# Square roots of ten chunks in pairs, four widths for the tail units, and a pair unit at the end

## The chip, the core and the metric

The kernel runs on one core of one Trainium2 chip. The metric is the device time of one execution in microseconds (us). TensorE (PE) multiplies into PSUM, ScalarE (ACT) applies functions and copies, VectorE (DVE) does element-wise work and scans, GpSimd (POOL) issues the scattered writes, SyncE (SP) issues the other transfers. Every engine has a queue of its own and takes its instructions in the order in which they stand there.

## What is computed

```python
a_base = sigmoid(a_param)
a_t = exp(8 * sigmoid(r_gate) * log(clip(a_base)))
x_gated = sqrt(max(1 - a_t * a_t, 1e-6)) * sigmoid(i_gate) * x
h_t = a_t * h_(t-1) + x_gated          # along 3648 steps, 4 sequences, 256 channels: y
group  = argmax(y @ w_group)           # 4 groups
expert = argmax(y @ w_expert[group])   # 4 experts in each: 16
out = weight_of_both_softmaxes * (relu(y @ w1[group, expert]) @ w2[group, expert])
```

There are 14592 tokens of 256 channels; w1 is 256 x 1024 and w2 1024 x 256 for each of the 16 experts. A gated recurrence is scanned along time, and every token of its result goes through the one expert that a two-level router picks. Which expert that is stands in the data, so units of work take their expert and their rows from tables that the kernel makes as it runs.

## The kernel before

The program is not written in the order in which it runs. Functions such as `add_chunk` (the recurrence and the router of one chunk) and `add_unit` (an expert's two products for a group of rows) hand operations to a planner, each with its engine, a cost, a due time and the operations that it comes after. `plan.run` then emits the operations one by one: per engine, of those that can start about first, the one with the earliest due time. So a due time moves an operation against all others of its engine.

**Chunks.** The tokens pass in 16 chunks (sizes 4, 13 times 8, 4 and 2 blocks of 128 tokens), planned 16.5 us apart. With channels on partitions, there are two halves `h` of 128 channels. On ACT a chunk goes through tanh (`tanh_r`, L352), the exponential (`decay`, L357), the square (`square`, L365), the square root (`norm`, L371, both halves at once) and the input gate's tanh (`gate_i`, L375). tanh, exp and square are in one function table of ACT, the square root in another, so that the planner's order has a table load ahead of a root and one behind it, on the next tanh or exp. DVE then scales (`scale_s`, L383) and scans (`scan`, L394). PE turns the result into rows with the router's logits beside them (`rows1`), which ACT copies out of PSUM (`rows2`, L419) and POOL scatters to DRAM (L520), sorted by expert. The buffers `v` that hold squares and roots are four, two for a chunk.

**Units.** The rows of an expert are served in units. Eight resident blocks (L1154, L1170) and 12 "native" units run while chunks still pass. After these come 14 units of two blocks (256 rows) from tables made early, then 11 pair units from the table `tP` (two blocks each) and last 16 tails from the table `tT`, one for each expert, with two or three blocks that end at the expert's last row. A unit's four steps `j` have 12 products with W1 into PSUM (`mm1`, for a tail `mm1_tail`; three products for each of two halves of the channels, with high and low parts of the operands), the ReLU on ACT (L942) and its low part on DVE (L945), and then products with W2 into `q_o` (`mm2`). PE takes mm1 of step j ahead of mm2 of step j - 1. In a tail each of these is made for three blocks and for two, and the value `has3` picks one on each engine (`tail_if`, L965, behind one register load per engine and tail, L964). At the end of a unit `finish` scales each block out of `q_o`, on ACT and DVE, and `give` scatters it to the output (L1036, POOL). The tail of expert 15 is the last unit; its last step goes block by block, and its three results are planned as block 2, 0, 1.

Of the kernel before, what the change touches and what calls it, by code (L numbers as in the profile page):

```python
# [158 lines left out]
def rglru_moe_kernel(ctx: ExitStack, tc: tile.TileContext, x, r_gate, i_gate, a_param,  # L159
# [48 lines left out]
    ORES = 60  # L208
    HALVED = (2, 3, 4)
# [3 lines left out]
    IF = 0.3  # L213

# [354 lines left out]
    def add_chunk(ck, before):  # L569
# [11 lines left out]
        sq = {}  # L581
        for h in range(2):
# [5 lines left out]
        n2 = op("ACT", 2 * act(W), lambda: norm(ck), due + ONORM, [sq[0], sq[1]], use=[b["v", 0], b["v", 1]], table="sqrt",  # L588
# [15 lines left out]

        urgent = SOON if ck.c in URGENT else 0.0
# [203 lines left out]
    def tails():  # L809
# [34 lines left out]
    class Unit:  # L844
        def __init__(self, u, tb, t, due):
# [5 lines left out]
            self.final = tb is tT and t == NE - 1  # L851
            self.always = tb is tT or t < 2 or u < NATIVE + 2
# [8 lines left out]
    def load_weights(m, k):  # L861
# [11 lines left out]
        pool = "wf" if m.tb is tT else "x"  # L873
# [26 lines left out]
    def gather(m):  # L900
# [4 lines left out]
        if m.nb == 3:  # L905
            m.g = m.g[:, ::-1]

# [3 lines left out]
    def prep1(m, c):  # L911
        m.qx = pools["q_r"].tile([P, 512], F32, name="q_r")
        for h in range(m.nb):
            T.transpose(m.qx[:, h * P:(h + 1) * P], m.g[:, h, c * X1:c * X1 + P], ident)  # L914
# [32 lines left out]
    def mm1(m, j):  # L947
        m.qh = pools["q_h"].tile([P, 512], F32, name="q_h")
        for f in range(2):
            w1_products(m, j, f, m.qh[:, f * TS:(f + 1) * TS], TS)  # L950
# [20 lines left out]
    def mm1_tail(m, j):  # L971
# [6 lines left out]
        def body(N):  # L978
            for f in range(2):
                w1_products(m, j, f, q[f][:, :N], N)  # L980
        tail_if(m, ENG.PE, lambda: body(3 * P), lambda: body(2 * P))
        return q

    def relu_hi_tail(m, j, q):
        m.hh[j] = [pools["a"].tile([P, CH * P], F32, name="a").bitcast(F32R) for f in range(2)]

        def body(N):
            for f in range(2):
                relu1(m.hh[j][f][:, :N], q[f][:, :N])
        tail_if(m, ENG.Activation, lambda: body(3 * P), lambda: body(2 * P))  # L990

    def relu_lo_tail(m, j, q):
        m.hl[j] = [pools["i"].tile([P, CH * P], F32, name="i").bitcast(F32R) for f in range(2)]

        def body(N):
            for f in range(2):
                relu2(m.hl[j][f][:, :N], m.hh[j][f][:, :N], q[f][:, :N])
# [3 lines left out]
    def w2_products(m, j, hs):  # L1001
        tail = m.nb == 3
        steps = [(n, h) for n in range(3) for h in hs]
        if m.final and j == J - 1:
            steps = [(n, h) for h in sorted(hs, key=lambda h: (h + 1) % 3) for n in range(3)]
        for n, h in steps:
            for f in range(2):
                hx, w = (m.hl if n == 2 else m.hh)[j], (w2h, w2l, w2h)[n]
                mv = hx[f][:, h * P:(h + 1) * P] if tail else hx[:, f * TS + h * P:f * TS + (h + 1) * P]
# [218 lines left out]

    def add_results(m, bqs, due):
        for h in (2, 0, 1) if m.final else range(m.nb):  # L1230
            b = buf("o")
            bq = bqs[0]
            if h == 2:
                f_ = op("DVE", 0.5, lambda: finish(m, 2), due - HASTE, m.p2[-1:] + [m.oc], [b], [bq, m.bc])
            else:
# [270 lines left out]
```

## Time and profile before

| | |
|---|---|
| time, median of 3 runs | 898.94 us (898.26 to 898.94) |
| the profiled execution | 905.73 us, span 903.9 us |
| PE busy | 835.9 us (92%), 6288 matmuls |
| DVE busy | 661.9 us (73%) |
| ACT busy | 606.7 us (67%) |
| POOL busy | 288.3 us (32%) |

Busy times are unions of spans. Matmuls are pipelined: they start about 0.117 us (256 columns) apart and each is shown with a span of 0.28 us, so PE counts as busy over a gap of up to some 0.16 us, and a group is best timed from the start of its first matmul to the start of the next group. A wait is shown with the instruction that ended it. The last copy of a chunk's rows on ACT starts at 336.7 us, and the first tail's matmuls at 646 us.

### The profile page before, as it was taken

How to read it: one execution, taken by the hardware profiler on the slowest of the kernel's cores; microseconds unless marked ns; L12 is line 12 of the kernel's file. 1: busy time of each engine (PE TensorE's matmuls, PEld its weight loads, DVE VectorE, ACT ScalarE, POOL GpSimd, SP SyncE). 2: the span in 40 equal slices, each digit the busy share in tenths (PEclk: the TensorE clock that was granted, in tenths of full speed). 3: DMA queues.
4: the chain of work that ended last, by engine and by line, in shares of the span. 5: the costliest groups of instructions: out<-in, count | busy, mean ns of one | idle time of the engine just before them, and what ended most of it. 6: DMA issues, size and time to landing. Idle time of an engine off the chain costs nothing.

```text
span 903.9 us, 18963 instructions
## 1 busy us (share of the span) xinstructions
PE 835.9 (92%) x6288; PEld 809.3 (90%) x6288; DVE 661.9 (73%) x1351; ACT 606.7 (67%) x903; POOL 288.3 (32%) x290
## 2 busy tenths in 40 slices
PE   1459889999989989999999999999999999999994
PEld 1358779999879979999999999999999999999994
DVE  5897889888878846787777777778766666666671
ACT  9997989999879735655665555566555555555551
POOL 2326443663772557311111111111212212121132
PEclk9758999999999999999999999999999999999998
DMA  9998868999885677867777767788655656555420
GB/s 306 409 414 314 309 197 283 394 389 353 282 298 173 227 250 239 262 199 249 233 235 234 236 219 232 228 281 270 212 178 166 187 182 198 155 172 177 135 72 23
DMA packets 74462, 216.28 MB, mean 239 GB/s; under 512 B 10709, under 2 KB 28895, under 8 KB 71776
## 3 DMA queue, kind: packets, MB, share of 16 engines
q1 hardware_dynamic: 62464, 183.61, 61.6%
q0 software_dynamic: 11872, 31.10, 9.0%
q8 instruction: 66, 1.08, 0.5%
q14 instruction: 60, 0.49, 0.2%
HBM read 182.76 MB, written 34.00 MB: 240 GB/s over the span
## 4 chain that ended last, share of the span: by engine, by line
PE 77%; issue 5%; POOL 2%; ACT 1%; DVE 1%; DMA 0%; POOLq 0%; DVEq 0%; ACTq 0%
PE q_o L253 36%; PE q_h L253 29%; PE q_y L253 9%; PE q_r L914 2%; POOL out_dram L1036 1%; PE q_r L1108 0%; POOL y_s L520 0%; DMA y_s<-wf,pi 0%; ACT a L352 0%; ACT hh L1124 0%; ACT o L1028 0%; DVE o L1032 0%; ACT wf L419 0%; DVE v L383 0%; ACT a L357 0%
## 5 line engine op out<-in xcount | busy, mean ns | idle before, releaser
L1036 POOL DMA_INDIRECT out_dram<-o,cl x122 | 134.6, 1103 | 442.8 <-ACT o L1028 242.7
L253 PE MATMUL q_h<-xh,w1h 128*128 128x256 f32 (+1 forms) x720 | 186.6, 287 | 0.2 <-issue 0.2
L253 PE MATMUL q_h<-xh,w1l 128*128 128x256 f32 x592 | 164.7, 278 | 0.5 <-issue 0.5
L253 PE MATMUL q_h<-xl,w1h 128*128 128x256 f32 x592 | 164.5, 278 | 0.3 <-issue 0.3
L520 POOL DMA_INDIRECT y_s<-wf,pi x114 | 133.6, 1172 | 82.5 <-issue 35.0
L253 PE MATMUL q_o<-w2h,hh 128*128 128x256 f32 x784 | 156.5, 332 | 1.9 <-ACT hh L1124 1.3
L253 PEld LDWEIGHTS q_o<-w2h,hh 128*128 128x128 f32 x784 | 123.5, 189 | 10.1 <-ACT hh L1124 1.5
L253 PEld LDWEIGHTS q_h<-xh,w1h 128*128 128x128 f32 x720 | 126.8, 189 | 1.9 <-PE q_o L253 1.3
L942 ACT ACTIVATE hh<-q_h 128x512 fp32r<-128x512 f32 x100 | 60.1, 601 | 88.7 <-PE q_h L253 77.2
L253 PEld LDWEIGHTS q_h<-xh,w1l 128*128 128x128 f32 x592 | 111.1, 188 | 1.1 <-issue 1.1
L253 PEld LDWEIGHTS q_h<-xl,w1h 128*128 128x128 f32 x592 | 111.4, 188 | 0.7 <-issue 0.3
L945 DVE SCALAR_TENSOR_TENSOR hl<-q_h,hh 128x512 fp32r<-128x512 f32 x100 | 68.7, 688 | 46.6 <-ACT hh L942 44.9
L253 PE MATMUL q_y<-yw,a 128*128 128x148 f32 x360 | 60.8, 315 | 33.6 <-DVE a L394 25.1
L253 PEld LDWEIGHTS q_y<-yw,a 128*128 128x128 f32 x360 | 54.5, 208 | 38.7 <-issue 20.7
L253 PE MATMUL q_o<-w2l,hh 128*128 128x256 f32 x464 | 77.7, 293 | 1.1 <-ACT wf L419 1.0
L394 DVE TENSOR_TENSOR_SCAN a<-a,v 128x1024 f32<-128x1024 f32 (+8 forms) x44 | 68.9, 1581 | 0.4
L253 PEld LDWEIGHTS q_o<-w2l,hh 128*128 128x128 f32 x464 | 65.2, 189 | 2.8 <-ACT wf L419 1.2
L893 DVE TENSOR_TENSOR w1l<-x,w1h 128x1024 fp32r<-128x1024 f32 x50 | 61.0, 1221 | 6.3 <-ACT w1h L891 3.8
L942 ACT ACTIVATE a<-q_y 128x384 fp32r<-128x384 f32 (+1 forms) x64 | 25.0, 442 | 58.3 <-issue 32.8
L253 PE MATMUL q_o<-w2h,hl 128*128 128x256 f32 x400 | 62.9, 279 | 0.6 <-DVE hl L945 0.6
L893 DVE TENSOR_TENSOR w2l<-x,w2h 128x1024 fp32r<-128x1024 f32 x50 | 60.6, 1218 | 2.2 <-ACT w2h L891 2.2
L253 PE MATMUL q_h<-x,w1h 128*128 128x384 f32 (+1 forms) x256 | 58.7, 318 | 0.0
(300 smaller groups left out, 1846.5 us busy)
## 6 DMA issues: line engine op xcount, KB each, us to landing
x<-in_moe_w_dram SPq DMA_DIRECT2D x100, 512.0 KB
wf<-in_moe_w_dram SPq DMA_DIRECT2D x64, 512.0 KB
w2h<-in_moe_w_dram SPq DMA_DIRECT2D x14, 1024.0 KB
a<-in_r_gate_dram SPq DMA_DIRECT2D x26, 512.0 KB
i<-in_i_gate_dram SPq DMA_DIRECT2D x26, 512.0 KB
x<-in_x_dram SPq DMA_DIRECT2D x26, 512.0 KB
w2l<-in_moe_w_dram SPq DMA_DIRECT2D x24, 512.0 KB
g<-y_s SPq DMA_DIRECT2D x37, 276.0 KB
```

The lines of the kernel that those rows point to most:

```text
L253: last[0] = T.matmul(*a, **k).ins.name
L394: V.tensor_tensor_scan(a[:, sl], a[:, sl], v[:, sl], init, ALU.mult, ALU.add)
L520: ins = G.indirect_dma_start(out=y_s, out_offset=bass.IndirectOffsetOnAxis(ap=ck.pi[:, k:k + 1], axis=0), in_=ck.t["yo", k // 4][:, k % 4, ...
L893: V.tensor_tensor(lo[m.b][:, sl], src, hi[m.b][:, sl].bitcast(F32), op=ALU.subtract)
L914: T.transpose(m.qx[:, h * P:(h + 1) * P], m.g[:, h, c * X1:c * X1 + P], ident)
L942: S.activation(hh, q, AF.Relu)
L945: V.scalar_tensor_tensor(hl, q, 0.0, hh.bitcast(F32), op0=ALU.max, op1=ALU.subtract)
L1036: ins = G.indirect_dma_start(out=out, out_offset=bass.IndirectOffsetOnAxis(ap=m.col("idx", h), axis=0), in_=m.o[h], in_offset=None, bounds ...
```

## The change

Three things are changed. First, chunks 5, 7, 9, 11 and 13 get the due times of their recurrence 8 us later, and the chunk behind each of them gets its own 8 us sooner; besides, the square root of the first chunk of a pair may only be placed once both squares of the second are placed. Rows and routing of the first chunk are due 8 us later too, those of the second as before; loads keep their due times.

Second, a tail holds its rows at the end of its 384 columns, the empty ones ahead of them (`m.at`), and how many are empty is kept in a table `room`. PE loads that number at a tail's first step and picks the columns of the W1 products by it: with 128 or more empty rows the last 256 columns; else the first product over all 384, and the other five from column 0, 32, 64 or 96 on. ACT and DVE still choose between two and three blocks. The chain of DVE that makes the tails' tables is due 150 us later.

Third, the last pair unit comes behind the tails. It always loads its weights, into the tails' buffers `wf`, and its last step is two operations of PE, one for each block, with the block's result and scatter placed right after each.

```diff
+    PAIRS, SOONER, LATER = (5, 7, 9, 11, 13), 8, 8
+    TRIM = 32
+    LATE = 150
...
         sq = {}
+        mid = due
+        due += (ck.c in PAIRS) * LATER - (ck.c - 1 in PAIRS) * SOONER
...
-        n2 = op("ACT", 2 * act(W), lambda: norm(ck), due + ONORM, [sq[0], sq[1]], use=[b["v", 0], b["v", 1]], table="sqrt",
+        if ck.c - 1 in PAIRS:
+            for h in range(2):
+                before.n2.wait += 1
+                sq[h].then.append(before.n2)
+        n2 = ck.n2 = op("ACT", 2 * act(W), lambda: norm(ck), due + ONORM, [sq[0], sq[1]], use=[b["v", 0], b["v", 1]], table="sqrt",
...
+        due = mid + (ck.c in PAIRS) * LATER
...
+        tT.room = small([1, NE], I32)
+        V.tensor_copy(tT.room, nv[0:1, :])
...
-            self.final = tb is tT and t == NE - 1
-            self.always = tb is tT or t < 2 or u < NATIVE + 2
+            self.final = tb is tP and t == NPS - 1
+            self.always = tb is tT or self.final or t < 2 or u < NATIVE + 2
...
+        m.at = [slice((m.nb - 1 - h if m.nb == 3 else h) * P, (m.nb - h if m.nb == 3 else h + 1) * P) for h in range(m.nb)]
...
-    def w1_products(m, j, f, q, N):
+    def w1_products(m, j, f, q, wide, lo, hi):
...
-                matmul(q, lhsT=w[m.b][:, c, fs], rhs=mv[:, c, :N], start=n == 0, stop=n == 5)
+                a = wide if n == 0 else lo
+                matmul(q[:, a:hi], lhsT=w[m.b][:, c, fs], rhs=mv[:, c, a:hi], start=n == 0, stop=n == 5,
+                       skip_group_check=wide < lo)
...
+        def body(wide, lo):
+            for f in range(2):
+                w1_products(m, j, f, q[f], wide, lo, 3 * P)
+
+        def classes(lo, hi):
+            if lo == hi:
+                return body(0, lo * TRIM)
+            mid = (lo + hi) // 2
+            with tc.If(m.room > mid * TRIM + TRIM - 1) as cmp:
+                classes(mid + 1, hi)
+            with cmp.Else():
+                classes(lo, mid)
+        if j == 0:
+            m.room = nc.values_load(tT.room[0:1, m.t:m.t + 1], min_val=0, max_val=HEAD, engines=[ENG.PE])
+        with tc.If(m.room > P - 1) as cmp:
+            body(P, P)
+        with cmp.Else():
+            classes(0, P // TRIM - 1)
...
-        tail_if(m, ENG.PE, lambda: body(3 * P), lambda: body(2 * P))
...
         def second(j):
+            if m.final and j == J - 1:
+                for h in range(2):
+                    m.p2.append(op("PE", 6 * B, lambda h=h: w2_products(m, j, (h,)), due + STEP2, seq[-1:] + [rl[j], ws[3]], use=bh[j] + [bo],
+                                   order=m.left))
+                    seq.append(m.p2[-1])
+                    add_result(m, h, bo, due + STEP2)
+                return
...
-    tT.row = chain(tails(), [0.18] * 6 + [0.2] * 3, due, [eP])[1]
+    tT.row = chain(tails(), [0.18] * 6 + [0.2] * 3 + [0.18], due + LATE, [eP])[1]
...
-    kinds = [(tb, t) for tb, (_, n) in zip(tAs, STAGES) for t in range(n)] + [(tP, t) for t in range(NPS)] + [(tT, t) for t in range(NE)]
+    kinds = [(tb, t) for tb, (_, n) in zip(tAs, STAGES) for t in range(n)] + [(tP, t) for t in range(NPS - 1)] + [(tT, t) for t in range(NE)] + [(tP, NPS - 1)]
```

What the due times do to the order shows on ACT. Before, around the square root of chunk 5 (L371 is the root, L352 tanh, L375 the gate's tanh, L1158 and L1170 the resident blocks' copy and ReLU, L419 the copies of rows):

```order
L1158 COPY xh<-q_r 128x256
L375 ACTIVATE i<-i 128x1024
L371 ACT_TABLE_LOAD
L371 ACTIVATE v<-v,la 128x1024 x2
L1170 ACTIVATE hh<-q_h 128x512
L352 ACT_TABLE_LOAD
L352 ACTIVATE a<-a 128x1024
L419 COPY wf<-q_y 128x552
```

The same place on ACT after the change, where lines have moved down (root L374, tanh L355, gate L378, square L368, blocks L1185 and L1197, the router's exponential L444):

```order
L368 ACTIVATE v<-a 128x1024
L444 ACTIVATE d__985<-d__985 128x160
L378 ACTIVATE i<-i 128x1024
L374 ACT_TABLE_LOAD
L374 ACTIVATE v<-v,la 128x1024 x2
L1197 ACTIVATE hh<-q_h 128x512
L374 ACTIVATE v<-v,la 128x1024 x2
L1185 COPY xh<-q_r 128x256
L1197 ACTIVATE hh<-q_h 128x512
L355 ACT_TABLE_LOAD
L355 ACTIVATE a<-a 128x1024 x2
```

The roots of chunks 5 and 6 stand behind one load, with chunk 6's tanh, decay, square and gate ahead of both. The whole program lists 27 table loads on ACT for 35: for chunks 11 and 12 a router's exponential stands between the two roots.

On PE, inside one step's W1 products of the first tail, before: the end of the body for three blocks and the start of the one for two, with the jump between them.

```order
L253 MATMUL q_h<-x,w1h_4358 128x384 x2
L253 MATMUL q_h<-x,w1l_4359 128x384
L965 UNCONDITIONAL_BRANCH
L253 MATMUL q_h<-x,w1h_4358 128x256 x2
L253 MATMUL q_h<-x,w1l_4359 128x256
```

The same place on PE after the change (L1007 is the test for 128 empty rows, L1001 the tests between the four other widths): the end of the body for two blocks, and the first half of the next.

```order
L256 MATMUL q_h<-x,w1l_4145 128x256
L1007 UNCONDITIONAL_BRANCH
L1001 COMPARE_AND_BRANCH x2
L256 MATMUL q_h<-x,w1h_4144 128x384
L256 MATMUL q_h<-x,w1h_4144 128x288
L256 MATMUL q_h<-x,w1l_4145 128x288
L256 MATMUL q_h<-x,w1h_4144 128x288 x2
```

Where two bodies stood there are five, with three tests on the way to any of the last four; PE's list grows from 7362 rows to 9665.

On PE at the end of the planned units, with waits, before: the last step's W2 products of the last tail, in the body for two blocks.

```order
L965 UNCONDITIONAL_BRANCH
L253 MATMUL q_o<-w2h_4170,a 128x256 [waits Activation_49] x2
L253 MATMUL q_o<-w2l_4170,a 128x256 x2
L253 MATMUL q_o<-w2h_4169,i 128x256 [waits DVE_49] x2
L253 MATMUL q_o<-w2h_4169,a 128x256 x2
L253 MATMUL q_o<-w2l_4170,a 128x256 x2
L253 MATMUL q_o<-w2h_4169,i 128x256 x2
```

And after the change, the last step of the pair unit that now comes last:

```order
L256 MATMUL q_o<-w2h_4146,hh 128x256 [waits Activation_49] x2
L256 MATMUL q_o<-w2l_4147,hh 128x256 x2
L256 MATMUL q_o<-w2h_4146,hl 128x256 [waits DVE_49]
L256 MATMUL q_o<-w2h_4146,hl 128x256
L256 MATMUL q_o<-w2h_4146,hh 128x256 [waits Activation_49]
L256 MATMUL q_o<-w2h_4146,hh 128x256
L256 MATMUL q_o<-w2l_4147,hh 128x256 x2
L256 MATMUL q_o<-w2h_4146,hl 128x256 x2
```

Both go block by block; the second block's first product has a wait for ACT now, which it had not.

## Rows read from the trace of the kernel before

**Rows 1.** Busy time (and instructions) of each engine, granted clock, DMA, in five stretches.
```profile
core 0: us, PE busy (x) PEld busy (x) DVE busy (x) ACT busy (x) POOL busy (x), PEclk, DMA share, GB/s
80.00:140.00 60.00, 53.02 (x352) 48.56 (x353) 51.17 (x114) 54.94 (x68) 25.27 (x25) 0.97 0.71 251
140.00:300.00 160.00, 156.68 (x1065) 145.49 (x1064) 135.98 (x331) 146.29 (x196) 85.18 (x81) 1.00 0.87 310
300.00:360.00 60.00, 56.95 (x381) 52.60 (x380) 34.98 (x110) 31.52 (x54) 39.19 (x39) 1.00 0.69 231
650.00:892.00 242.00, 241.21 (x1818) 239.91 (x1816) 157.78 (x274) 126.74 (x229) 53.59 (x47) 1.00 0.52 158
860.00:892.00 32.00, 31.88 (x266) 31.32 (x264) 19.73 (x39) 15.24 (x32) 9.28 (x8) 1.00 0.18 57
```

**Rows 2.** PE's waits, 80 to 360 us: total, times, longest.
```profile
PE q_y L253 <- ACT wf L419: 3.9, 4, 2.0
...
PE q_o L253 <- ACT hh L1170: 1.6, 1, 1.6
...
PE q_o L253 <- ACT wf L419: 1.3, 2, 1.0
PE q_o L253 <- ACT hh L1124: 1.3, 1, 1.3
PE q_y L253 <- ACT w1h L1080: 0.9, 1, 0.9
...
PE q_r L1154 <- ACT v L371: 0.3, 1, 0.3
```

**Rows 3.** Lines L371 and L352 on ACT, 80 to 340 us: ns min/median/max.
```profile
L371 ACT ACT_TABLE_LOAD  x11: 1283/1283/1283, 89.9 to 301.9; - x11
...
L352 ACT ACT_TABLE_LOAD  x9: 1283/1283/1283, 93.9 to 295.2; - x9
```

**Rows 4.** ACT in order of time at chunk 5's root: start, us, instruction.
```profile
89.90 1.28 ACT L371 ACT_TABLE_LOAD   x1
91.19 2.19 ACT L371 ACTIVATE v<-v,la 128x1024 f32<-128x1024 f32 x2
```

**Rows 5.** PE in order of time, 94 to 100 us: idle time in brackets.
```profile
96.79 2.28 PE L253 MATMUL q_y<-yw,a 128*128 128x148 f32 x8 [2.04 <-ACT wf L419]
```

**Rows 6.** Matmuls by form, 650 to 892 us: busy us, mean ns of one.
```profile
L253 PE MATMUL q_h<-x,w1h 128*128 128x384 f32 x144 | 37.7, 343 | 0.0
...
L253 PE MATMUL q_h<-x,w1l 128*128 128x384 f32 x72 | 24.4, 339 | 0.0
```

**Rows 7.** A group of 12 (chain), then a two-block group's start and the next (time).
```profile
693.01 2.11 PE q_h L253 x12
...
649.04 0.40 PE L253 MATMUL q_y<-x,w1h 128*128 128x256 f32 x2
...
650.47 0.64 PE L253 MATMUL q_o<-w2h,a 128*128 128x256 f32 x4
```

**Rows 8.** Branches and register loads of PE's sequencer: ns min/median/max.
```profile
L965 PEldq COMPARE_BRANCH  x200: 65/177/372, 645.1 to 888.2; - x100
...
L964 PEldq TENSOR_LOAD <-sm x16: 299/305/492, 644.2 to 876.6; - x16
```

**Rows 9.** The queue of PE's instruction fetches on the page: packets, MB, share.
```profile
q8 instruction: 66, 1.08, 0.5%
```

**Rows 10.** The end in order of time, PE, ACT and POOL.
```profile
890.83 0.40 PE L253 MATMUL q_o<-w2h,i 128*128 128x256 f32 x2
...
891.54 0.40 PE L253 MATMUL q_o<-w2h,i 128*128 128x256 f32 x2
891.98 0.47 ACT L1028 ACTIVATE o<-q_o,cl 128x256 f32<-128x256 f32 x1 [2.13 <-PE q_o L253]
...
892.73 0.98 POOL L1036 DMA_INDIRECT out_dram<-o,cl  x1 [6.67 <-ACT o L1028]
...
895.30 0.98 POOL L1036 DMA_INDIRECT out_dram<-o,cl  x1 [0.30 <-issue]
```

More of the change, by code (lines that the diff above doesn't have):

```diff
@@ L949, in mm1 @@
         for f in range(2):
[L950 removed]
+            w1_products(m, j, f, m.qh[:, f * TS:(f + 1) * TS], 0, 0, TS)
         return m.qh
@@ L996, in body @@
             for f in range(2):
-                relu2(m.hl[j][f][:, :N], m.hh[j][f][:, :N], q[f][:, :N])
+                relu2(*(t_[:, 3 * P - N:3 * P] for t_ in (m.hl[j][f], m.hh[j][f], q[f])))
         tail_if(m, ENG.DVE, lambda: body(3 * P), lambda: body(2 * P))
@@ L1003, in w2_products @@
         steps = [(n, h) for n in range(3) for h in hs]
-        if m.final and j == J - 1:
-            steps = [(n, h) for h in sorted(hs, key=lambda h: (h + 1) % 3) for n in range(3)]
         for n, h in steps:
@@ L1008, in w2_products @@
                 hx, w = (m.hl if n == 2 else m.hh)[j], (w2h, w2l, w2h)[n]
-                mv = hx[f][:, h * P:(h + 1) * P] if tail else hx[:, f * TS + h * P:f * TS + (h + 1) * P]
+                mv = hx[f][:, m.at[h]] if tail else hx[:, f * TS + h * P:f * TS + (h + 1) * P]
                 matmul(m.qo[h], lhsT=mv, rhs=w[m.b][:, 2 * j + f, :], start=j == f == n == 0 and h < 2,
@@ L1227, in add_blocks, with add_result @@
         pend(1)
-    def add_results(m, bqs, due):
[L1230 to L1235, printed above, removed]
-                f_ = op(*(("ACT", 0.47) if h == 0 else ("DVE", 0.48)), lambda h=h: finish(m, h), due - HASTE, m.p2[-1:] + [m.oc], [b],
-                        [bq, m.bc])
-            step = [] if m.native else None
-            g_ = op("POOL", 1.15, lambda h=h, step=step: give(m, h, step), due, [f_], use=[b, m.bc], dma=P * D * 4)
-            g_.step = step
+    def add_result(m, h, bq, due):
+        b = buf("o")
+        f_ = op(*(("ACT", 0.47), ("DVE", 0.48), ("DVE", 0.5))[h], lambda: finish(m, h), due - HASTE, m.p2[-1:] + [m.oc], [b], [bq, m.bc])
+        m.left = [f_]
+        step = [] if m.native else None
+        g_ = op("POOL", 1.15, lambda: give(m, h, step), due, [f_], use=[b, m.bc], dma=P * D * 4)
+        g_.step = step
+    def add_results(m, bqs, due):
+        for h in range(m.nb):
+            add_result(m, h, bqs[0], due)
     def add_native(m, before):
@@ L1310, in add_unit @@
         for k in range(4):
-            wf = buf("wf" if tail else "x")
+            wf = buf("wf" if tail or m.final else "x")
             lw = op("SP", 0.1, lambda k=k: load_weights(m, k), early, [m.tb.row],
@@ L1318, in add_unit @@
             hi_ = op("ACT", 1.05 + IF * (not m.always), lambda k=k: split_weights(m, k, 0), at, [lw] + used + free, use=[wf],
-                     order=wh[-1:] + (before.rh[k:k + 1] if tail else []))
+                     order=wh[-1:] + (before.rh[k:k + 1] if tail or m.final else []))
             wh.append(hi_)
             ws.append(op("DVE", 1.22 + IF * (not m.always), lambda k=k: split_weights(m, k, 1), at, [hi_], use=[wf],
-                         order=before.rl[k:k + 1] if tail else ()))
+                         order=before.rl[k:k + 1] if tail or m.final else ()))
         bg = buf("v" if tail else "g")
@@ L1361, in add_unit @@
         bh = {}
+        m.left = []
         for j in range(J):
```

8 lines of the change are left out of this document (3 added, 5 removed).

## The prediction

> **What bounds the kernel now.** I read the busy time by stretch first [rows 1]. TensorE (PE) is the engine to look at: in 650 to 892, the stage of the tails, it is busy 241.21 of 242 us at the full granted clock (1.00, the 2.4 GHz level), while ScalarE (ACT) and VectorE (DVE) are at 52% and 65%. So in that stage a microsecond is won only by giving PE fewer columns, or behind PE's last matmul. Between 80 and 360 the picture is another: ACT is busy 146.29 of 160 us in 140 to 300, yet PE is busy 156.68 of the same 160, because matmuls of the native units fill in while the chunks pass through ACT. PE's idle time from 80 to 360 is 6.98 + 3.32 + 3.05 = 13.4 us, and that is all that a faster ACT can give. The list of PE's waits there [rows 2] splits it: those that ACT ended are 3.9 + 1.6 + 1.3 + 1.3 + 0.9 + 0.3 = 9.3 us. The stretch before 80 us is left alone, since the change begins with chunk 5. The sum below is made against the profiled execution's span, 903.9 us; it took 905.73 us in all, against a median of 898.94, so a microsecond of the one counts as one of the other (0.7% apart). A measurement of this kernel can tell about 0.2% (1.8 us) from no change.
>
> **Pairs of square roots, ACT's side.** A switch to the square root's table and one back cost 1283 ns each: from 80 to 340 there are 11 loads ahead of square roots and 9 ahead of tanh [rows 3], 20 x 1.283 = 25.7 us, and the ACTIVATE behind a load starts as the load ends (89.90 + 1.28 = 91.18 against 91.19 [rows 4]). Ten would go if all five pairs joined. The order of instructions shows 27 loads in the whole program for 35: one router exponential stands between the roots of chunks 11 and 12, and that pair saves nothing. So ACT is relieved of 8 x 1.283 = 10.3 us.
>
> **Pairs, PE's side.** ACT's 10.3 us lie beside PE's work, not on it. They count only where PE waited for ACT, so the gain is at most 9.3 us [rows 2]. Against it stands what the pairing delays: chunk 5's roots now stand behind tanh, decay, square and gate of chunk 6 on ACT, some eight instructions of about 1 us each (a root of a half takes 2.19 / 2 [rows 4], and these have the same shape). Behind them wait, on DVE, scale and scan of chunk 5 (and then all four scans of a pair in one run), on PE its rows, and on ACT the copies of these. Who would feel it is PE, if it has no other matmuls by then. The nearest rows for that price are waits of the same kind: PE waited for a row copy 3.9 + 1.3 us in six waits, the longest of them (2.04, at 96.79) behind chunk 5's roots and the load back for tanh [rows 2, 4, 5]. Doubling them costs 5 us. Between -9.3 and +5 I take -3: the copies of chunk 4's rows no longer have a load, two roots and a load back in front of them [rows 4], which is the place of the longest wait; but ACT stays an in-order queue that is nine tenths full, and what no longer waits for it may wait for DVE, 135.98 of 160 us busy. Both ends are kept for the range. The input loads keep their dates; with the rows move the router's steps on DVE and the scatters on GpSimd (POOL, 85.18 of 160 us busy), which nobody needs before the next stage's table.
>
> **Four widths for the tails, the columns.** A tail's second operand is up to 384 columns wide. Counting the tokens of each expert with the reference's inputs, and taking off what residents, early stages and pairs have served, nine of the sixteen tails have three blocks. The profile agrees: 144 + 72 matmuls of 384 columns into q_h [rows 6], and as many into q_y (two rows that repeat these), are 432 = 9 x 48. Their empty rows, rounded down to 32, are 32, 0, 96, 0, 32, 32, 32, 0, 32: 256 columns together. Of the six products into one PSUM bank the first stays 384 wide, five are cut; with 4 steps and 2 banks that is 40 matmuls a tail, so 256 x 40 = 10240 columns fewer. Price of a column: a group of 12 matmuls takes 2.11 us at 384 columns and 650.47 - 649.04 = 1.43 us at 256 [rows 7]; 0.68 us / (12 x 128) = 0.443 ns. The new widths lie between these two, so the trim is worth 10240 x 0.443 = **4.5 us**, all of it on PE, which has no cover there. The seven two-block tails keep 256. What is late next in these tails: the products with W2 wait for the ReLU of the step before, on ACT and DVE, and the group of W1 products between is its cover; at 288 columns, the narrowest, that cover shrinks from 2.11 to 1.68 us, still above the 1.43 that two-block tails live with.
>
> **Four widths, the branches.** A three-block group had one test not taken and one jump; now it has three tests, and a register load per tail comes on top. Branches ran on PE's sequencer 65 to 372 ns, median 177, 200 of them, and 16 loads took 305 [rows 8]: 35.4 + 4.9 = 40 us, while PE idled 0.8 us in the whole stage [rows 1]. The sequencer works them off while matmuls that it issued before still run. The change adds about 0.4 us of tests and jumps to each of 36 groups of the three-block tails (two more of 0.177 at the median), 0.07 to 28 others and 16 loads of 0.3: 21 us, at a visible share of 0.8 / 40 some **+0.4 us**. The least is 0 (no branch goes, so no gain), the most 21 us if nothing were hidden; I stay at the low end since these are the same instructions in the same places.
>
> **The fetch.** The added bodies lengthen PE's program from 7362 listed rows to 9665, and jumps now skip up to four bodies. In the rows, instruction fetch is 66 packets on its queue with 0.5% of 16 engines' time [rows 9], 0.005 x 16 x 904 / 66 = 1.1 us each, and no jump of before cost PE as much. The Trainium skill (Runtime: NRT & Kernel Launch, section on instruction fetch mechanics) says that a taken branch to a target outside the current window of two pages forces a fetch before execution goes on. By that rule the added jumps could show themselves; by the rows they do not. It is a rival below.
>
> **A two-block unit comes last.** Nothing in the number of matmuls changes; the last pair unit moves behind the sixteen tails, with its four weight loads, its gather on SP's queue, four splits on ACT and four on DVE. They go past the tails' 64 loads; the DMA engines are busy for 18% of 860 to 892 [rows 1], so nothing collides. It always loads now, as it did before (its expert differs from that of two units earlier). The end does change [rows 10]. Before: PE ends at 891.94, ACT's result at 892.45, then three scatters on POOL of 0.98 with 0.30 between, 892.73 to 896.28; the third block is empty in this tail, and is sent all the same. Now there are two, and the last step's products come block by block. Call E0 the end of block 0's six matmuls (891.23 on before's clock). ACT's result ends at E0 + 0.51, and PE's block 1 waits for it (the order lists a wait for ACT there): six matmuls until about E0 + 1.5, DVE's result E0 + 2.0, its scatter E0 + 2.28 to 3.26; the first scatter, from E0 + 0.79, is out of the way by 2.07. Before it was E0 + 5.05. Gain **1.8 us**. What follows the last scatter (7.6 us of drains) stays. The tails' table of DVE is put 150 us later; the first tail starts at 646, so it is hidden.
>
> **Sum.** -3 -4.5 + 0.4 -1.8 = -8.9 us; 898.9 - 8.9 = **890.0 us**.
>
> **Rivals.** *A, slower:* the pairing starves PE between 100 and 340. Its place is the first row copy of each pair, its price one longest wait (2.04 us) for each of five pairs, 10.2 us instead of -3: 898.9 - 5.9 + 10.2 = 903.2. It decides once PE's idle time from 80 to 360 passes 13.4 + 5.9 = 19.3 us. For it: an in-order DVE that is 85% busy gets four scans in a run. Against: PE idles 3.3 of the 160 us from 140 to 300 [rows 1], which says that native units stand ready. Chance 0.09. *B:* ACT's relief takes all waits for ACT: -9.3 - 5.9, 883.7. Chance 0.13. *C:* the idle time only changes places (0 to +4): 893 to 897. Chance 0.15. *D:* fetches show: if half of the 64 groups paid 1.1 us, +35 us, about 925. Chance 0.03. *E:* the change does not do what it says, matmuls of 288 to 352 columns cost what 384 cost: 894.5. Chance 0.05.
>
> **How the numbers follow.** The forecast, 890 with a few microseconds to either side, has 0.55. The range 883.5 to 897.5 takes in B's value, C and E, and leaves A, D and the far side of B out, 0.15 or so. Faster by over 0.2% are the forecast, B, E and most of C: 0.85; within 0.2% the rest of C: 0.05; slower A and D with a remainder: 0.10.
>
> **What would show it.** Right: 27 table loads on ACT; PE idle for 8 to 13 us from 80 to 360; in the tail stage groups of 12 matmuls of 2.11, 1.97 and 1.68 us and PE's idle time under 1.5 us; two scatters behind the last matmul, the last ending some 3 us behind block 0's. Wrong: PE's idle time in the chunk stage over 19 us, gaps in PE behind tests in the tails, or groups that stay at 2.11 us whatever their width.

## The result and the profile after

The changed kernel takes **907.36 us** (903.96 to 909.99, six runs), the kernel before beside it 898.95 (898.26 to 901.44): a ratio of **1.0081, 95% interval 1.0065 to 1.0097**. It is slower; forecast were 890.0 us and a range of 883.5 to 897.5. The runs below came in five more batches, in which the kernel before took 888.4 to 902.1 us, so every ratio here is against the kernel before in the same batch. The median of `pairs_44` below leaves out one execution of 1706.97 us, far off all its others.

The stretches of [rows 1] in the profile after (span 904.5 us):

```profile
core 0: us, PE busy (x) PEld busy (x) DVE busy (x) ACT busy (x) POOL busy (x), PEclk, DMA share, GB/s
80.00:140.00 60.00, 53.49 (x351) 48.80 (x351) 43.60 (x104) 46.97 (x61) 26.84 (x24) 0.94 0.63 215
140.00:300.00 160.00, 155.29 (x1049) 144.68 (x1048) 135.23 (x313) 144.84 (x196) 91.49 (x81) 1.00 0.89 323
300.00:360.00 60.00, 56.16 (x376) 51.87 (x375) 38.79 (x136) 28.21 (x50) 33.07 (x36) 1.00 0.62 213
...
650.00:892.00 242.00, 240.05 (x1847) 238.33 (x1846) 160.82 (x279) 130.17 (x232) 55.42 (x48) 1.00 0.51 163
```

ACT is relieved as foreseen (27 table loads; 46.97 busy against 54.94 from 80 to 140), but PE's idle time from 80 to 360 is 6.51 + 4.71 + 3.84 = 15.1 us: not less than the 13.4 of [rows 1]. PE's waits from 80 to 360, to be held against [rows 2]:

```profile
PE q_y L256 <- ACT wf L422: 5.5, 5, 1.7
PE q_o L256 <- ACT hh L1197: 3.5, 2, 3.3
PE q_h L256 <- issue: 1.4, 2, 0.9
```

PE still waits for ACT. Waits for a row copy (`wf`) into q_y have grown from 3.9 to 5.5 us.

### The profile page after: what moved, and what is told of

The parts are those of the page before. It is cut to its first block, busy times and chain, and to the rows that moved or that the text cites. A ratio compares the mean times of both kernels' runs of the same rounds, so it can differ in the third digit from the quotient of the medians.

```text
span 904.5 us, 19053 instructions
## 1 busy us (share of the span) xinstructions
PE 833.9 (92%) x6288; PEld 806.2 (89%) x6288; DVE 660.2 (73%) x1352; ACT 596.7 (66%) x895; POOL 296.2 (33%) x290
## 4 chain that ended last, share of the span: by engine, by line
PE 81%; ACT 10%; DMA 3%; issue 2%; DVE 2%; another core or an unknown queue 1%; SPq 0%; DVEq 0%; POOLq 0%; POOL 0%; ACTq 0%
PE q_o L256 39%; PE q_h L256 29%; PE q_y L256 10%; PE q_r L927 2%; ACT v L374 2%; ACT a L355 1%; ACT a L360 1%; ACT i L378 1%; DMA i<-in_i_gate_dram 1%; DMA a<-in_r_gate_dram 1%; DMA x<-in_moe_w_dram 1%; ACT L374 1%; ACT wf L422 1%; ACT v L368 1%
## 5 line engine op out<-in xcount | busy, mean ns | idle before, releaser
L1063 POOL DMA_INDIRECT out_dram<-o,cl x122 | 142.4, 1167 | 431.0 <-ACT o L1055 246.4
L256 PE MATMUL q_h<-xh,w1h 128*128 128x256 f32 (+1 forms) x720 | 188.5, 289 | 1.4 <-issue 1.4
L256 PE MATMUL q_y<-yw,a 128*128 128x148 f32 x360 | 58.8, 308 | 33.5 <-DVE a L397 25.2
L905 DVE TENSOR_TENSOR w1l<-x,w1h 128x1024 fp32r<-128x1024 f32 x48 | 58.6, 1221 | 6.0 <-ACT w1h L903 3.7
L1057 DVE TENSOR_SCALAR o<-q_o,cl 128x256 f32<-128x256 f32 x53 | 25.6, 484 | 48.6 <-ACT o L1055 30.0
L905 DVE TENSOR_TENSOR w2l<-x,w2h 128x1024 fp32r<-128x1024 f32 x48 | 58.0, 1216 | 2.6 <-ACT w2h L903 2.6
```

The source lines that it names most:

```text
L256: last[0] = T.matmul(*a, **k).ins.name
L905: V.tensor_tensor(lo[m.b][:, sl], src, hi[m.b][:, sl].bitcast(F32), op=ALU.subtract)
L1057: V.tensor_scalar(o, m.qo[h], m.col("cw", h), None, op0=ALU.mult)
L1063: ins = G.indirect_dma_start(out=out, out_offset=bass.IndirectOffsetOnAxis(ap=m.col("idx", h), axis=0), in_=m.o[h], in_offset=None, bounds ...
```

## The experiments

The forecast's sum had three parts: pairing (-3), the tails' columns and branches (-4.5 + 0.4), the end (-1.8). The first question is which part went wrong.

### Each part alone

`pairs_only` is the kernel before with the pairing lines alone. `tails_last` is the changed kernel without them, and `last_only` has one body a case besides, so that only the last unit's place is left:

```diff
 tails_last, against the changed kernel
-    PAIRS, SOONER, LATER = (5, 7, 9, 11, 13), 8, 8
+    PAIRS, SOONER, LATER = (), 8, 8
 last_only, besides
-    TRIM = 32
+    TRIM = 128
```

`before_again` is the kernel before, unchanged, for a second trace.

> The kernel before, unchanged, for a second profile of it. The changed kernel measured 907.4 us against 898.9 (+8.4), but the two profiled executions lie only 0.6 us apart (spans 904.5 and 903.9), since the profiled execution of before took 905.7 us, 6.8 more than the timed ones. If that one execution was slow by chance, this profile's span is near 897 and PE's idle time from 80 to 360 us is some 6 us below the 13.4 of the first profile. If a profile always costs this kernel 7 us, the span is near 904 again and the idle time near 13.

> The kernel before with the paired square roots alone; tails and the last unit as before. Theory P (the pairing starves PE in the chunk stage, rival A of the prediction): the whole loss is here, and more, since tails and end gained about 4 us in the trace of after: 910 to 914 us, PE idle over 16 us from 80 to 380. Theory T (the branches and fetches of the tails eat more than the narrower widths give): 894 to 900 us here. Theory L (the unit that comes last or the later tables of the tails): 894 to 900 us as well.

> The changed kernel without the pairing: four widths in the tails and the pair unit last. Theory P: 893 to 896 us (columns -4.5, end -1.8 to -2, less 1.5 to 2 for a fetch and the waits at the end). Theory T or L: 903 to 909 us.

> As tails_last, with the trim's step at 128 columns: one width of 384 for three-block tails, one test on the number of empty rows, and the pair unit last. Theory P: 2.5 to 4.5 us above tails_last, 897 to 899 us. Theory T: 4 us or more below tails_last, 899 to 903. Theory L: the same as tails_last, 903 to 909.

| kernel | us | ratio to before (95%) | end of the last row copy, us |
|---|---|---|---|
| before_again | 889.17 | 0.9998 (0.9989 to 1.0007) | 322.5 |
| pairs_only | 896.28 | 1.0083 (1.0070 to 1.0096) | 328.5 |
| tails_last | 885.72 | 0.9957 (0.9945 to 0.9969) | 322.0 |
| last_only | 888.38 | 0.9987 (0.9978 to 0.9996) | 322.1 |

The last column is the end of the last L419/L420/L422 copy of a chunk in the profiled execution. Pairing costs 7.0 us and all the rest of the change gains 3.6. The added tail bodies are worth 885.72 - 888.38 = -2.7, the last unit -0.9. **tails_last is faster than both kernels** (its interval lies below 1). The loss is pairing's, as its theory said, though less than expected there.

The trace of before_again bears on what the forecast was built on. Its stretches from 80 to 360:

```profile
80.00:140.00 60.00, 56.84 (x401) 52.45 (x401) 55.28 (x129) 58.12 (x72) 28.16 (x26) 1.00 0.79 276
140.00:300.00 160.00, 160.00 (x1092) 149.96 (x1092) 139.82 (x338) 150.26 (x204) 94.20 (x87) 1.00 0.85 310
300.00:360.00 60.00, 60.00 (x437) 57.13 (x436) 40.38 (x111) 31.86 (x50) 35.48 (x36) 1.00 0.83 274
```

PE's waits in it from 75 to 360 (total, times, longest):

```profile
PE q_o L253 <- ACT wf L419: 1.9, 2, 1.0
PE q_y L253 <- ACT wf L419: 0.6, 1, 0.6
PE q_y L253 <- DVE t L759: 0.4, 1, 0.4
PE q_r L1154 <- ACT xh L1158: 0.3, 1, 0.3
```

The same program, with the same order of instructions, leaves PE idle for 3.2 us here and for 13.4 in [rows 1]. In this execution, from 140 to 360, there is not one microsecond that a faster ACT could give.

Two things differ between the two traces. The profiled execution of the forecast had taken 905.73 us against a timed median of 898.94, 6.8 more. And its batch was at another level: the kernel before took 898.95 us in the first comparison and 902.12 and 901.33 in two batches below, but 889.28, 888.42 and 889.04 in the other three. At the upper level such idle time is usual. `tails_wide` (below) has the chunk stage of the kernel before and ran where that took 902.12; its profiled execution, 903.15, lies at its kernel's median (903.71):

```profile
80.00:360.00 280.00, 269.13 (x1828) 250.08 (x1827) 225.15 (x557) 235.49 (x319) 152.58 (x146) 0.99 0.80 283
```

That is 10.9 us of idle time, of which waits that ACT ended are 8.2. So most of the 13.4 goes with the level, and not with one untypical execution. The levels part ahead of the first paired root. The same ReLU of a resident block on ACT, in the traces of before, tails_wide and before_again:

```profile
80.80 0.60 ACT L1170 ACTIVATE hh<-q_h 128x512 f32<-128x512 f32 x1 [4.10 <-remote]
80.10 0.60 ACT L1197 ACTIVATE hh<-q_h 128x512 f32<-128x512 f32 x1 [3.88 <-PE q_y L256]
77.37 0.60 ACT L1170 ACTIVATE hh<-q_h 128x512 f32<-128x512 f32 x1 [0.76 <-PE q_h L253]
```

All eight traces from batches at the upper level have such a wait of ACT, 3.8 to 4.4 us up to some 80.5 us, and one of DVE of 2.5 to 3.2 us that ends with it; in the twelve from the lower level ACT waits there for at most 0.8 us. What causes it, no run shows. It does not go by the chip's number: chip 14 is on record for the batch at 889.04 and for the one at 901.33.

pairs_only in the batch of before_again, PE's waits from 75 to 360:

```profile
PE q_y L254 <- ACT wf L420: 6.3, 4, 2.0
PE q_o L254 <- ACT wf L420: 0.9, 3, 0.4
```

And ACT's waits there that a DMA ended:

```profile
ACT a L353 <- DMA a<-in_r_gate_dram: 6.6, 2, 3.9
ACT wf L420 <- DMA y_s<-wf,pi: 3.2, 1, 3.2
ACT w1h L1088 <- DMA w2l<-in_moe_w_dram: 1.6, 3, 0.8
ACT i L376 <- DMA i<-in_i_gate_dram: 0.7, 1, 0.7
```

before_again has 1.4 us of such DMA waits (0.8, 0.4 and 0.2). From 74 to 293 us, the columns of [rows 1], before_again:

```profile
74.00:293.00 219.00, 215.84 (x1489) 201.61 (x1489) 193.83 (x473) 208.43 (x275) 120.97 (x115) 1.00 0.86 310
```

And pairs_only:

```profile
74.00:293.00 219.00, 213.58 (x1453) 198.80 (x1453) 183.15 (x432) 195.97 (x263) 126.12 (x111) 0.99 0.86 309
```

ACT has 12.5 us less to do (208.43 - 195.97) and yet ends its last root at 292.6 us against 293.2: **the time won stands there as waiting**. The row copies come later and PE is fed later. What follows the last row copy took 567.4 us in the profiled executions of both kernels (889.86 - 322.5, 895.93 - 328.5), so pairing's loss is all in front of it.

### Is it the late input loads?

ACT waits for r-gate loads. SP issues them late, behind i-gate loads that wait for a buffer (SP's waits for a buffer of i from 75 to 340 are 12.0 us against 1.6, and the second half of chunk 8's r-gate is issued at 121.5 us against 99.5). If that is the cause (theory Q), the loads have to come sooner, or the buffers to be more. `after_again` is the changed kernel once more, to be held against the sum of its parts.

```diff
 pairs_loads, against pairs_only
-                    at = due + LOADS[what] + 3 * h
+                    at = due + LOADS[what] + 3 * h - (ck.c - 1 in PAIRS) * SOONER * (what == "a")
 pairs_i6 and before_i6, against pairs_only and the kernel before
-    BUFS = dict(i=4, x=4, a=8,
+    BUFS = dict(i=6, x=4, a=6,
```

> The changed kernel itself, on the chip on which its parts were timed, where the kernel before takes 889.2 us. If the parts add up (pairing +7.0; trim and last unit together -3.6): 892.6 us, a ratio of 1.004. If pairing and tails cost each other something (the pairs delay the router's table or the tails' weights), or if the first chip was no exception: 896 us, the ratio of 1.008 of the first comparison. What tells them apart beside the time: the stretch from 650 to the end should be 2 to 4 us shorter than in the kernel before in either case.

> Pairing alone, but the r-gate loads of each pair's second chunk are due 8 us sooner on SP's queue, as its tanh is. (The order of ACT then has 29 table loads, 2 more than pairing alone: +2.6 us of ACT time at most.) Theory Q (late loads: SP holds the r-gate loads behind i-gate loads that wait for buffers which a pair keeps longer; ACT stands for them, and the row copies behind): ACT's waits for in_r_gate from 80 to 340 fall from 6.6 us to under 2, PE's waits for row copies from 6.3 to under 3, and the time goes from 896.3 to 890 to 893. Theory S (the pair itself bunches the work of two chunks ahead of the row copies; late loads are a side effect): 895 to 898 whatever becomes of the loads.

> Pairing alone, with 6 buffers of i (gates and scaled inputs) instead of 4, at the cost of two of the 8 buffers of a. To be compared with the kernel before with the same buffers. Theory Q: a pair no longer makes the next i-gate loads wait, r-gate loads come up in time, ACT's waits for input loads from 80 to 340 fall from 8.9 us (6.6 + 1.6 + 0.7) to under 3, and the time is at most 2.5 us above the kernel before with the same buffers. Theory S: it stays 6 to 8 us above that kernel, with PE waiting some 2 us for the row copies at the pairs.

> The kernel before with 6 buffers of i and 6 of a, for comparison with pairing under the same buffers. Both theories: 887 to 892 us, since PE stands idle only 3 us from 80 to 360 in the kernel before and no load there is waited for by more than 1.2 us in all; more than 894 would say that a needs its 8 buffers, and then the pair with 6 is no test.

Measured, with the kernel before at 888.42 us: after_again 891.74, ratio 1.0044 (1.0031 to 1.0057): the parts add up. pairs_loads 895.73, 1.0082 (1.0069 to 1.0095): no gain. pairs_i6 912.27, 1.0264 (1.0250 to 1.0277); before_i6 891.65, 1.0043 (1.0028 to 1.0058). By the times theory Q falls. Theory S fits pairs_loads (895 to 898), but not pairs_i6: it gave 6 to 8 us over before_i6, and 20.6 were measured. pairs_loads' trace tells more. ACT's waits for input loads, 75 to 360:

```profile
ACT i L376 <- DMA i<-in_i_gate_dram: 8.9, 3, 7.4
ACT a L353 <- DMA a<-in_r_gate_dram: 4.4, 4, 3.1
```

ACT in order of time, with idle time in brackets:

```profile
126.67 1.06 ACT L376 ACTIVATE i<-i 128x1024 f32<-128x1024 f32 x1 [7.43 <-DMA i<-in_i_gate_dram]
...
131.56 0.61 ACT L420 COPY wf<-q_y 128x552 f32<-128x552 f32 x1
```

And PE:

```profile
132.22 2.34 PE L254 MATMUL q_y<-yw,a 128*128 128x148 f32 x8 [4.40 <-ACT wf L420]
```

The r-gate came sooner, and ACT stood for the i-gate instead, 7.43 us, with the row copy behind it and PE waiting 4.40 us for that copy. In pairs_i6 it is the other way round: i has buffers enough, a has not, and ACT stood 21.1 us for r-gate loads. The expected recovery failed both times. The way from a late load to ACT, to the row copy, to PE is seen; that the loads are the whole cause is not, since both kernels moved the wait rather than took it away.

### What is a microsecond of ACT worth, and how much is one pair?

`before_block` puts 13 small squares of a scratch tile on ACT ahead of the tanh of chunks 6, 8, 10, 12 and 14 in the kernel before. `pairs_44` and `pairs_three` vary the pairs. `tails_wide` has all tail bodies and tests, each computing all 384 columns.

```diff
 before_block, against the kernel before, in tanh_r
+        if ck.c in (6, 8, 10, 12, 14) and h == 0:
+            for _ in range(13):
+                S.activation(spin, spin, AF.Square)
 pairs_44, against pairs_only
+    PAIRS, SOONER, LATER = (5, 7, 9, 11, 13), 4, 4
 pairs_three, against pairs_only
+    PAIRS, SOONER, LATER = (5, 9, 13), 8, 8
 tails_wide, against tails_last
-                return body(0, lo * TRIM)
+                return body(0, 0)
```

> The kernel before with ACT made to spend about 2.5 us more (13 small squares of a scratch tile, which nothing reads) ahead of the tanh of chunks 6, 8, 10, 12 and 14: as much in all (12.5 us) as ACT stood waiting in the pairing kernel, at the same chunks, with the table loads all still there. Theory B: an in-order ACT that is held up for 2 to 4 us ahead of row copies is what PE feels; PE waits for row copies at two to five places and 3 to 8 us are lost: 892 to 897. Theory S: PE has native units ready in this order of work, a hold of 2.5 us on ACT costs at most 1.5 us in all (889 to 890.7), and the loss of the pairing kernel is in its order of work.

> Pairing alone, with the second chunk's tanh, decay and square 4 us sooner instead of 8 and the first chunk's roots 4 us later instead of 8 (also 27 table loads). Theory B (a pair holds all four buffers of i and of v until its joint roots, the next chunks' loads can't be issued in that time, and ACT, in its order, stands for them, with the row copies behind): ACT is asked for the next loads later, so its waits for input loads and for wf from 75 to 380 fall from 12.1 us to 5 to 8, and the loss from 7.0 to 2 to 5: 891 to 894 us. Theory S (each pair costs by itself, since the row copies of two chunks stand behind the steps of both): 895 to 897, as with 8 and 8.

> Pairing of three pairs, 5+6, 9+10 and 13+14, with two single chunks between pairs (29 table loads, three fifths of the relief). Theory B: behind a single chunk's roots its own two buffers come free, so the next pair finds some of its loads issued in time; loss under 2 us, 888 to 891, with ACT's waits for input loads under 4 us. Theory S: three fifths of 7.0, +4.2: 893.4 us, with three PE waits of about 2 us for row copies.

> The four bodies and three tests of the tails and the last unit, without pairing, but every body computes all 384 columns: the tests and bodies without the columns they save. Against the kernel with one width (888.4 us) it gives the price of the tests and bodies by themselves, against the kernel with trimmed bodies (885.7) the worth of the columns. Theory F (the added bodies cost fetches that PE sees): 889.5 to 890.5, so that columns are worth 4.1 to 4.5 as forecast and the tests 1.4. Theory W (columns between 256 and 384 are worth less than forecast, and the tests cost nothing): 888.4.

The kernel before took 902.12 us here. before_block: 917.93, 1.0164 (1.0137 to 1.0191), +14.8 us by the ratio. The added work on ACT (instructions, busy us, mean ns):

```profile
L357 ACT ACTIVATE spin<-spin 128x16 f32<-128x16 f32 x65 | 14.1, 216 | 1.9
```

And PE's waits in it from 75 to 360:

```profile
PE q_y L253 <- ACT wf L425: 14.7, 7, 5.1
PE q_o L253 <- ACT wf L425: 4.3, 2, 4.1
```

14.1 us more on ACT cost 14.8 (12.4 to 17.2 by the interval), more than either theory gave: **holding ACT up ahead of row copies cost about its full length, while the time that pairing takes off ACT brought nothing**. pairs_44 takes 915.36, 1.0128 (1.0093 to 1.0164), and pairs_three 912.28, 1.0105 (1.0078 to 1.0133): both lose, and more than either theory gave them. Five pairs with 8 and 8 were not run alone in this batch, so it is not shown whether the milder shift, or two pairs fewer, saves anything. pairs_three has no wait for an input load at all, and loses as well. Late loads are one way to the loss and not its condition: theory B, which made them that, falls.

tails_wide, 903.71, 1.0023 (1.0001 to 1.0045), is read in its own stage. From the first tail's transposes to PE's last matmul, with the last unit in, last_only, tails_wide and tails_last:

```profile
598.98:876.68 277.70, 276.43 (x2118) 274.80 (x2116) 183.43 (x312) 148.45 (x262) 61.19 (x55) 1.00 0.54 167
610.77:891.52 280.75, 277.26 (x2118) 274.82 (x2116) 183.42 (x312) 148.40 (x262) 61.22 (x55) 1.00 0.51 165
599.26:875.36 276.10, 272.52 (x2118) 269.80 (x2116) 183.44 (x312) 148.38 (x262) 62.17 (x55) 1.00 0.52 168
```

(The level matters little there: without the last unit this stage took 265.0 us in the execution of the forecast and 265.1 in before_again.) The tests and bodies cost 3.1 us, the columns are worth 4.7. These are single executions; by the ratios of the whole kernels the two are 3.2 and 5.9. Theory F holds, with a higher price than it gave. In this stage PE idles 3.5 us in tails_wide, 3.6 in tails_last and 1.3 in last_only. Branches of the changed kernel's L1001 and L1007 (ns, least, median, most):

```profile
L1001 PEldq COMPARE_BRANCH  x96: 65/208/2007, 650.3 to 838.2; - x96
...
L1007 PEldq COMPARE_BRANCH  x92: 65/208/1361, 638.2 to 877.1; - x92
```

The one of 2007 ns starts at 807.2 us, and PE felt it:

```profile
809.55 0.62 PE L256 MATMUL q_h<-x,w1h 128*128 128x384 f32 x2 [1.07 <-issue]
```

The most in [rows 8] was 372. The Trainium skill (Runtime: NRT & Kernel Launch, section on instruction fetch mechanics) has a taken branch out of the window wait for a fetch; the trace agrees as far as branches of up to 2007 ns go. That these are fetches is not shown: the 85 fetch packets for 66 [rows 9] grow no more than PE's list does, 9665 rows for 7362. Most of the time in branches lies beside issued matmuls.

### Every pair, or one?

pairs_four leaves out the last pair; pair_first, pair_last and, in the last batch, pair_7 have one pair; pairs_rest leaves out the first; pairs_again is pairs_only.

```diff
 against pairs_only: pairs_four, pair_first, pair_last, pairs_rest, pair_7
+    PAIRS, SOONER, LATER = (5, 7, 9, 11), 8, 8
+    PAIRS, SOONER, LATER = (5,), 8, 8
+    PAIRS, SOONER, LATER = (13,), 8, 8
+    PAIRS, SOONER, LATER = (7, 9, 11, 13), 8, 8
+    PAIRS, SOONER, LATER = (7,), 8, 8
```

> Pairing of four pairs, without the last, 13+14 (29 table loads, eight us of ACT relief). What follows the last row copy took 563 to 574 us in every profiled execution so far, so the loss has to be read from when that copy ends. Theory E (the order at the end of the chunk stage: a pair that holds rows back just before the last chunks leaves more row copies behind the last root, and earlier pairs cost nothing lasting): the last row copy ends no later than in the kernel before, ratio 0.997 to 1.001. Theory S (every pair costs, its delay is carried along from pair to pair): four fifths of the loss of five pairs on the same chip, ratio 1.005 to 1.008.

> The first pair alone, 5+6 (33 table loads, 2.6 us of ACT relief). Theory E: there are 200 us of chunk stage behind it in which ACT can give back what the pair cost, ratio 0.998 to 1.001. Theory S: a fifth of the loss of five pairs or more, ratio 1.0015 to 1.004, with the roots of all later chunks later than in the kernel before.

> The last pair alone, 13+14 (33 table loads). Theory E: nearly the whole loss of five pairs, 5 to 8 us, ratio 1.005 to 1.009, with the roots up to chunk 12 at the dates of the kernel before and the last row copy 5 us or more later. Theory S: a fifth, ratio 1.001 to 1.003.

> All five pairs once more, on the chip of the three kernels beside it, as their measure. Both theories: ratio 1.008 to 1.011 (it was 1.0083 where the kernel before took 889 us).

| kernel | us (before there) | ratio (95%) | last row copy | PE idle, 74 us to it |
|---|---|---|---|---|
| pair_first | 895.10 (889.04) | 1.0074 (1.0060 to 1.0088) | 327.4 | 7.4 |
| pair_last | 889.24 (889.04) | 1.0001 (0.9992 to 1.0010) | 322.0 | 3.2 |
| pairs_four | 893.70 (889.04) | 1.0059 (1.0046 to 1.0073) | 328.1 | 5.7 |
| pairs_again | 895.58 (889.04) | 1.0089 (1.0073 to 1.0104) | 327.3 | 6.7 |

One pair, 5+6, costs 6.1 us, nearly as much as five. The last pair, on which theory E had put the loss, costs nothing. Theory S, which gave either of them about a fifth of the loss, fits neither. The last pair doesn't win either: its last root ends at 288.0 us against 293.2 in before_again, 5 us sooner, and the last row copy at 322.0 as before, because PE has no gap to close (140 to 300, pair_last):

```profile
140.00:300.00 160.00, 160.00 (x1091) 149.98 (x1090) 139.05 (x334) 149.17 (x203) 99.25 (x88) 1.00 0.87 311
```

pair_first can be read instruction by instruction. PE around chunk 5's first rows (`q_y<-yw,a` and `q_o<-yw,a`):

```profile
124.14 1.17 PE L254 MATMUL q_y<-yw,a 128*128 128x148 f32 x8
125.15 1.95 PE L254 MATMUL q_h<-xh,w1h 128*128 128x128 f32 x16
126.94 1.17 PE L254 MATMUL q_o<-yw,a 128*128 128x148 f32 x8
127.94 0.60 PE L1116 MATMUL q_r<-yw,g 128*128 128x128 f32 x4
133.57 2.15 PE L254 MATMUL q_y<-yw,a 128*128 128x148 f32 x8 [5.03 <-ACT wf L420]
135.52 2.73 PE L254 MATMUL q_o<-w1l,hh 128*128 128x256 f32 x8
138.09 1.95 PE L254 MATMUL q_h<-xh,w2h 128*128 128x128 f32 x16
```

ACT at the same time:

```profile
122.45 1.06 ACT L353 ACTIVATE a<-a 128x1024 f32<-128x1024 f32 x1 [2.86 <-DMA a<-in_r_gate_dram]
124.48 1.06 ACT L376 ACTIVATE i<-i 128x1024 f32<-128x1024 f32 x1 [0.97 <-DMA i<-in_i_gate_dram]
...
130.34 2.19 ACT L372 ACTIVATE v<-v,la 128x1024 f32<-128x1024 f32 x2
132.44 0.57 ACT L1178 ACTIVATE hh<-q_h 128x512 f32<-128x512 f32 x1
132.91 0.61 ACT L420 COPY wf<-q_y 128x552 f32<-128x552 f32 x1
```

The first of chunk 5's copies in before_again:

```profile
108.33 0.61 ACT L419 COPY wf<-q_y 128x552 f32<-128x552 f32 x1
```

There the rows stand on PE at 106 us and are copied at 108.33. Held back for the pair, they are ready at 125.3, and their copy now stands on ACT behind a tanh and decay of chunk 8 and a gate, the squares, the table load and the roots that follow, and two of these wait 3.8 us for loads (the DMA engines are busy for 29% of 100 to 110 us, 72% in before_again, and all of the time from 123 to 138). So the copy comes at 132.91, 24.6 us later. PE has used up what else was issued to it by 128.5 and waits 5.03 us for q_y, of which there is one buffer. The wait has a tail (six and four microseconds from 128 and 134):

```profile
128.00:134.00 6.00, 0.97 (x7) 0.74 (x6) 1.71 (x2) 5.98 (x9) 0.00 (x0) 0.98 1.02 406
134.00:138.00 4.00, 4.00 (x15) 3.54 (x15) 3.68 (x6) 3.65 (x6) 0.13 (x1) 0.60 1.02 395
```

Behind the gap the granted clock is 0.60 on average, so most of the 4 us are at the 1.2 GHz level. The eight products into q_y and the eight into q_o behind the gap take 1.95 and 2.57 us from start to start; at the full clock the same forms take 1.01 (at 124.14) and 1.73 us: 1.8 us more. With 7.4 us of idle time for 3.2 that makes 6.0 of the 6.1 us that this pair costs.

> The four later pairs without the first, 7+8, 9+10, 11+12 and 13+14 (27 table loads, as with all five). Theory G (the loss belongs to the place of pair 5+6: there the next steps of ACT wait for r-gate and i-gate loads and PE has no native unit's products left to do, so the row copies of chunk 5 are waited for once, 5 us, and the roots of all later chunks stay late): without it the ratio is 0.997 to 1.002. Theory H (any pair that is followed by many chunks costs this, whichever comes first): 1.005 to 1.009, with a PE wait of 4 us or more between 130 and 170 us.

> The pair 7+8 alone, 33 table loads as with 5+6 alone. Theory G: ratio 0.998 to 1.002, the roots of chunk 9 and later at the dates of the kernel before or sooner. Theory H: ratio 1.005 to 1.009, as 5+6 alone (1.0074), with one long wait of PE for the row copies of chunk 7.

The last batch ran where the kernel before took 901.33 us. pairs_rest: 911.91, 1.0122 (1.0100 to 1.0144). pair_7: 912.25, 1.0133 (1.0111 to 1.0155). Theory G, which gave the loss to the place of 5+6, falls. Theory H has the direction right: a pair that is followed by many chunks costs, here as with 5+6, and further pairs add little. But both ratios lie above its 1.005 to 1.009, and its long wait of 4 us is in neither trace: the longest of PE's waits is 2.3 us in pairs_rest and 3.2 us in pair_7, both put down to issue. This batch is at the upper level and that of pair_first at the lower, so the prices of 7+8 and 5+6 can't be held against each other. In pair_7 PE's waits are many, and its idle time from 74 us to the last row copy is 17.4 us, against 10.9 in tails_wide, which has the chunk stage of the kernel before and ran where that took 902.12.

**What stays open:** why a first pair costs nearly all and the next ones little, what holds ACT in pair_7, where it waits 8.0 us that the profile puts down to nothing, and what puts a batch at one level or the other.

## Why the prediction was wrong, point by point

- **What bounds the kernel, and -9.3 as the most to be gained [rows 1, 2].** The waits were read from one execution that took 6.8 us longer than the median, and the text set that aside as 0.7%. As a bound for the batch of the forecast the 9.3 was still near (8.2 in tails_wide, a usual execution at that level); at the lower level PE idles for 3.2 us in all, and there was next to nothing to win. The bound is not the step that failed: pairing loses at both levels.
- **Pairs, ACT's side:** right. 27 table loads, 10.3 us. In pairs_only they came back as waiting.
- **Pairs, PE's side, -3: the step that failed**, by 10 us at the lower level (pairs_only +7.0; +6.1 with one pair). It counted on chunk 5's rows being held back by some eight instructions of 1 us, and on PE having other products meanwhile; in pair_first they were copied 24.6 us later, and PE ran out of products at 128.5 us. Its price for delayed row copies was the waits of that kind doubled, 5 us, none of them longer than 2.04 [rows 5]; pair_first has one of 5.03, pairs_loads one of 4.40, and the clock behind such a wait was left out. "The copies of chunk 4's rows no longer have a load, two roots and a load back in front of them" was true, but what stood in front of chunk 5's copies was a whole chunk's work. "The input loads keep their dates" was wrong: their due times stayed, but SP issued the second chunks' r-gate loads up to 22 us later.
- **Columns, -4.5:** right, 4.7 between tails_wide and tails_last in their stage.
- **Branches, +0.4:** 3.1 by last_only and tails_wide, inside the bounds 0 to 21, at the wrong place in them. "The same instructions in the same places" left out the new bodies: rival D, if the long branches are fetches, came in small, a few of 1 to 2 us and one or two of them felt, not half of 64.
- **The end, -1.8:** about right, 1.7. The two scatters:

```profile
893.78 0.98 POOL L1063 DMA_INDIRECT out_dram<-o,cl  x1 [5.76 <-ACT o L1055]
...
895.37 0.98 POOL L1063 DMA_INDIRECT out_dram<-o,cl  x1 [0.61 <-DVE o L1057]
```

The second ends at 896.35, 3.35 us behind block 0's end at 893.00, where the forecast had 3.26 and before 5.05. The whole of the last unit gave 0.9 us (last_only), with an interval from 0.4 to 2.0, which does not tell it from 1.7.
- **Rival A** (0.09, 903.2) named the mechanism and the place, the first row copy of a pair, and its price per wait is that of three of the four waits in pairs_only (1.98, 1.97 and 1.83 us). Its point of decision, 19.3 us of idle time, was counted from an execution 6.8 us above its median; the changed kernel is slower at 15.1.

The sum with measured terms, at the lower level: +7.0 for pairing and -3.6 for the rest, +3.4; after_again measured +3.3 by the medians. The first comparison, at the upper level, has +8.4. Pairs cost more there (9.5 to 12.0 us by the ratios of pairs_44, pairs_three, pairs_rest and pair_7). If the rest gains 3.6 there too, which no run shows, the five pairs cost 12.0 in the first comparison, the upper end of these.

## What to carry to other kernels

Before waits are read as something to be won, hold the profiled execution's own time against the timed median, and profile the unchanged kernel in another batch: the idle time that was to be won here was 13.4, 10.9 and 3.2 us in three traces of the same stage. Where an engine that is full is fed by an in-order engine, relieving the feeder gives no more than the waits that are there, while regrouping its work is paid at the first hand-over that comes late (6.1 us for one pair here), with the clock behind it. So ask of a batching change not how much of the feeder's time it saves, but what stands in the feeder's queue in front of the first item that the full engine waits for.

## What the runs showed of the hardware

- One idle stretch of 5.03 us on PE was followed by 4 us at a granted clock of 0.60, in which sixteen matmuls took 1.8 us longer than the same forms at 1.00.
- Branches of PE's sequencer took up to 2007 ns once the tails had five bodies (372 before). PE idled about 1 us for the longest of these.
- The same program took 888.4 to 889.3 us in three batches and 899 to 902 us in three others, two of them, one of each kind, under the same chip number. The traces from the upper level share a wait of ACT of 3.8 to 4.4 us up to some 80.5 us; PE's idle time from 80 to 360 us was 3.2 us at the lower level, 10.9 and 13.4 at the upper.
